# Expert weights of a PEER layer: half of the one-hot's product with the gate given to GpSimd

## The chip, the cores and the metric

The kernel runs on one core of one Trainium2 chip. The metric is the device time of one execution in microseconds (us); the time of a kernel is the median of its runs. The engines of the core are named as in the profile: PE (matrix products, with its weight loads as PEld), DVE (the vector engine), ACT (the scalar engine), POOL (GpSimd) and SP (which issues most of the DMAs). Each runs its own queue of instructions in order, and semaphores make one wait for another.

## The reference

One transformer block over 2048 tokens of width 448: layer norm, attention with 16 heads, a residual, then a second layer norm and a PEER layer (a mixture with one expert per row of `u` and `v`, 64 x 64 = 4096 experts). What matters here is the PEER layer:

```python
s1 = einsum("nhd,ed->nhe", q1, k1); s2 = einsum("nhd,ed->nhe", q2, k2)
i1 = argsort(-s1)[..., :8];  i2 = argsort(-s2)[..., :8]
cand = t1[..., :, None] + t2[..., None, :]          # 64 pairs per head
top_s, top_e = best 8 of cand, expert = i1 * 64 + i2
g = softmax(top_s)
act = gelu(einsum("nd,nhkd->nhk", xf, u[top_e]))
out = einsum("nhk,nhk,nhkd->nd", g, act, v[top_e])
```

So each token has 16 heads x 8 = 128 chosen experts, each with a gate.

## The kernel before

The kernel doesn't gather rows of `u` and `v`. It computes all 4096 expert activations of a token as dense products and multiplies them by a dense table of gates, `G`, that is zero where an expert wasn't chosen. The tokens go through the PEER layer in four batches of 512 (`b` = 0 to 3). For each batch:

- `up` (L1208 for its load, L100 for its 11 matmuls, L1221 for the GELU) computes the activations of 128 experts, `f` = 0 to 31.
- `weights` (L1019 to L1086) builds `G` for the batch.
- `weigh` (L1261, with L1267 to L1270) multiplies the activations by `G` and the scale and splits the product in two f16 parts; `experts` (L1273, matmuls on L1295) multiplies these by `v` into the four accumulators `acc`; `drain` (L1302, L1305) adds the residual and writes the batch out.

`weights` is the part around the change. The 128 chosen slots of a token lie on the partitions. A chosen expert has a number split in two: a row of 128 and a column of 32. The table of one token is then a product of two one-hot matrices over the slots: a 128-wide one, `p1`, and a 32-wide one, `f1`, whose ones are replaced by the gates. The gate is kept as a high f16 part (`k` = 0) and a low f16 part (`k` = 1), so there are two versions of the gated one, side by side in the tile `fg` with the shape [128, 16, 2, 32, 2]: pairs of tokens, part `k`, column, token of the pair.

The work goes in steps of 16 tokens (`TG`), and in groups of 32 (`TF`), two steps each. On DVE:

- `first(t)` (L1035) makes `f1` for a group by comparing the slots' columns with an iota; 1024 elements per partition. The tile has one buffer (tag `f1`).
- `factors(t, f1)` (L1041) multiplies `f1` by both parts of the gate, 2048 elements per partition, into `fg`, which has two buffers.
- `chosen(s)` (L1049) runs once a step. At the first step of a group it calls `factors`; at the second it calls `first` for the next group; in both it then makes `p1` for its step (L1056; 2048 elements, two buffers).

The loop of `weights` calls `chosen` one step ahead: at step `s` it first issues `chosen(s + 16)` and then the matmuls of step `s`. For batch 0 these are two matmuls of 32 columns per token (L1083), added up on PE, and ACT copies the result to `G` (L1085). For the batches 1 to 3 it is one matmul of 64 columns per token (L1073), and the two parts are added by ACT and DVE: ACT copies the high part from PSUM to `G` (L1076), and DVE adds the low part, read from PSUM, to it (L1077), twice a step.

The order around the change: batch 0 is woven with other work by hand (`weave` inside a `manual_schedule` block, L1228 on): the projection of batch 3, `kept_scores` (matmuls on L100 into the tile `M`, copies by ACT) and the first `up`s. For the later batches the program weaves `weights(b + 1)` in two parts. The first `2 + EARLY` pieces (`EARLY` is 11, 11 and 13 of the 32 steps) run beside the end of `experts(b)`; the rest runs beside 19 `up`s of the next batch and the `drain` of the last (L1322). There a planner orders the instructions of each engine, with some orders pinned (`issue_after`). `G` of a batch must be complete before its first `weigh` past the ones in flight, because each expert's slice takes all 512 tokens.

Of the kernel before, what the change touches and what calls it, by code (L numbers as in the profile page):

```python
# [12 lines left out]
F16 = mybir.dt.float16  # L13
# [3 lines left out]
OP = mybir.AluOpType  # L17
# [47 lines left out]
def block(ctx: ExitStack, tc: tile.TileContext, x, wqk, wv, wo, wq, k12, uT, v, cst, out):  # L65
    nc = tc.nc
# [931 lines left out]
    TG = 16  # L998
    TF = 32
# [16 lines left out]
    def of_tokens(b, c):  # L1016
        return G[:, :, TG * c:TG * c + TG] if b % 2 == 0 else G[:, c].rearrange("p (f t) -> p f t", t=TG)

    def weights(b, summed=(), name=lambda: "A"):  # L1019


        st = bg.tile([128, 2, 1024], F16, name="st", bufs=2)
        nc.sync.dma_start(st, s_d[b])
        slots, gslots = st[:, 0].rearrange("p (k n) -> p k n", k=2), st[:, 1].rearrange("p (t k u) -> p t k u", k=2, u=2)

        def pairs(k, t, m, n):
            return (slots[:, k, t:t + m].rearrange("p (t u) -> p t u", u=2).unsqueeze(2)
                    .to_broadcast([128, m // 2, n, 2]))

        def ids(m, n):  # L1030
            return iota2[:, :n].unsqueeze(1).to_broadcast([128, m // 2, n, 2])

        def first(t):
            f1 = bk.tile([128, TF // 2, 32, 2], F16, name="f1", tag="f1")
            nc.vector.tensor_tensor(f1, pairs(1, t, TF, 32), ids(TF, 32), op=OP.is_equal)  # L1035
            return f1

        def factors(t, f1):
            fg = gp.tile([128, TF // 2, 2, 32, 2], F16, name="fg", bufs=2)
            g = gslots[:, t // 2:t // 2 + TF // 2].rearrange("p t k u -> p (t k) u")  # L1040
            nc.vector.tensor_tensor(  # L1041
                fg.rearrange("p t k f u -> p t k (f u)"),
                f1.rearrange("p t f u -> p t (f u)").unsqueeze(2).to_broadcast([128, TF // 2, 2, 64]),
                g.unsqueeze(2).to_broadcast([128, TF, 32, 2]), op=OP.mult)
            return fg

        f1 = fg = None

        def chosen(s):  # L1049
            nonlocal f1, fg  # L1050
            if s % TF == 0:
                fg = factors(s, f1)
            elif s + TG < 512:
                f1 = first(s + TG)
            p1 = bk.tile([128, TG // 2, 128, 2], F16, name="p1", tag="p1", bufs=2)
            newest[0] = nc.vector.tensor_tensor(p1, pairs(0, s, TG, 128), ids(TG, 128), op=OP.is_equal).ins  # L1056
            return p1, fg

        yield
        f1 = first(0)  # L1060
        ahead = chosen(0)
        yield
        for s in range(0, 512, TG):
            p1, f = ahead
            if s + TG < 512:
                ahead = chosen(s + TG)
            dst = of_tokens(b, s // TG)
            if s // TG in summed:
                for h in range(0, TG, TG // 2):
                    ps = P[0].tile([128, TG // 2, 2, 32], F32, name=name())  # L1070
                    for t in range(TG // 2):
                        a, u = divmod(h + t, 2)
                        nc.tensor.matmul(ps[:, t], p1[:, a, :, u], f[:, s % TF // 2 + a, :, :, u], start=True, stop=True)  # L1073
                    hi, lo = (ps[:, :, k].rearrange("p t f -> p f t") for k in range(2))
                    d = dst[:, :, h:h + TG // 2]
                    nc.scalar.activation(d, hi, AF.Copy)  # L1076
                    nc.vector.tensor_tensor(d, lo, d, op=OP.add)  # L1077
            else:
                ps = P[0].tile([128, TG, 32], F32, name=name())
                for t in range(TG):  # L1080
                    a, u = divmod(t, 2)
                    for k in range(2):
                        nc.tensor.matmul(ps[:, t], p1[:, a, :, u], f[:, s % TF // 2 + a, k, :, u],  # L1083
                                         start=k == 0, stop=k == 1)
                nc.scalar.activation(dst, ps.rearrange("p t f -> p f t"), AF.Copy)  # L1085
            yield  # L1086
# [53 lines left out]
    with tc.manual_schedule(engines={ET.PE, ET.DVE, ET.Activation, ET.Pool, ET.SP}):  # L1140
# [31 lines left out]
        for b in range(3):  # L1172
            t = begin[b] - FOLDED
# [8 lines left out]
            else:  # L1182
                work += [(pipeline([pairs_of(j, nc.gpsimd) for j in (0, 1)], 6), 6 + PAIRS_POOL, t + 20, 257 - FOLDED)]
        w0 = weights(0)

        def first_tokens():
# [9 lines left out]
    gp = ctx.enter_context(tc.tile_pool(name="gp", bufs=1, side="right", reuse_waits="tile"))  # L1196
# [121 lines left out]
    for b in range(NB):  # L1318
        n = AHEAD if b else UP0
        if b:  # L1320
            tag[0] = "A"
            weave((ws, 32 - EARLY[b], 0, 1), (dr, 4, 0, 0.7), (ups(b, n), n, 0, 1))  # L1322
        acc = [pa.tile([128, 512], F32, name=f"acc{j}") for j in range(4)]
        work = [(experts(b, n, acc), 32, 0, 1)]
        if b == 0:
            tag[0] = "M"
            ws = weights(1, SUMMED[1], lambda: tag[0])
            work += [(islice(later, n), n, lo, hi) for n, lo, hi in ((2 * PAIRS, 0, 0.13), (32, 0.13, 0.6), (PLACES, 0.6, 0.72))]
            work += [(islice(ws, 2 + EARLY[1]), 2 + EARLY[1], 0.7, 1)]
        elif b < 3:  # L1330
            tag[0] = "M"
            ws = weights(b + 1, SUMMED[b + 1], lambda: tag[0])
            work += [(islice(later, LATER[b]), LATER[b], 0, SPLIT[b]), (islice(ws, 2 + EARLY[b + 1]), 2 + EARLY[b + 1], SPLIT[b] + 0.02, 1)]
        weave(*work)
        dr = drain(b, acc)
# [51 lines left out]
```

## Time and profile before

| | us |
|---|---|
| runs of the kernel before (three) | 1582.46, 1582.63, 1585.69 |
| median | 1582.63 |
| the profiled execution's own time | 1589.57 |
| its span in the profile | 1587.8 |

The profiled execution is 6.94 us above the median of the runs. All times within the trace are counted from the start of the span. By the trace, `weights` works on the four batches at these times, taken from the first and the last instruction on L1041: batch 0 from 829.5 to 914.6, batch 1 from 1036.9 to 1132.2, batch 2 from 1188.1 to 1296.1, batch 3 from 1350.9 to 1467.6. GpSimd's last instruction starts at 860.18 us; it does nothing in the rest of the kernel.

How to read it: the busy time of an engine says nothing by itself; what matters is which engine another one waits for in the stretch in question. The views of windows and of the chain of waits are therefore given stretch by stretch. A duration of an instruction is longer than the distance from its start to that of the next one on the same engine, since the end of one overlaps the start of the next; where DVE works without a pause, the distance between starts is what an instruction costs.

### The profile page before, as it was taken

To read this page: it belongs to the slowest core of one execution; us is meant where nothing else is said; L and a number is where in the kernel's file an instruction comes from. 1 tells how busy PE (TensorE), PEld (TensorE's weight loads), DVE (VectorE), ACT (ScalarE), POOL (GpSimd) and SP (SyncE) were. 2 spreads that over 40 slices of the span, in tenths; PEclk is the share of its full clock that TensorE was granted. 3 is DMA by queue.
4 is the path that set the end of the run, shared out by engine and by line. 5 is a ranking of instruction groups with operands and counts; after the bars stand their busy time and mean duration, and the time that the engine had idled before them with its cause. 6 is when DMAs were issued, how large, how long until landed. Compare 5 with 4: busy or idle time off the path is not lost.

```text
span 1587.8 us, 33145 instructions
## 1 busy us (share of the span) xinstructions
PE 1528.4 (96%) x12441; PEld 647.1 (41%) x12441; DVE 1168.6 (74%) x3944; ACT 907.6 (57%) x1220; POOL 360.4 (23%) x484
## 2 busy tenths in 40 slices
PE   5999999999999999999998999999999999999998
PEld 3444222222332233222335644455445554555444
DVE  7763355565667767666698999799998998889623
ACT  3544888898888888987863422334323343333321
POOL 1242000524245753796570000000000000000000
PEclk9999999999999999999999999999999999999999
DMA  8424688669965757678642244454344434443454
GB/s 277 141 98 127 220 270 262 203 196 296 298 214 160 202 180 226 197 199 270 222 139 89 72 145 129 130 179 117 107 136 137 150 98 148 130 136 113 121 144 134
DMA packets 176474, 270.36 MB, mean 170 GB/s; under 512 B 29948, under 2 KB 106492, under 8 KB 176312
## 3 DMA queue, kind: packets, MB, share of 16 engines
q1 hardware_dynamic: 172088, 266.14, 55.0%
q10 hardware_dynamic: 4224, 2.10, 0.5%
q8 instruction: 97, 1.59, 0.4%
q14 instruction: 65, 0.53, 0.1%
HBM read 215.91 MB, written 49.50 MB: 167 GB/s over the span
## 4 chain that ended last, share of the span: by engine, by line
PE 70%; DVE 22%; DMA 3%; POOL 2%; issue 2%; ACT 1%; SPq 0%; DVEq 0%; POOLq 0%; ACTq 0%
PE acc L1295 13%; PE A L652 13%; PE M L100 12%; PE S L574 11%; PE A L100 9%; PE pq L100 6%; DVE p L1056 4%; DVE G L1077 2%; DVE fg L1041 2%; PE M L280 2%; DVE ring L1267 1%; DVE pos L880 1%; DVE w L1270 1%; DVE f L1035 1%; PE A L1083 1%
## 5 line engine op out<-in xcount | busy, mean ns | idle before, releaser
L578 ACT ACTIVATE P<-S,escale 128x1024 f32<-128x1024 f32 x512 | 533.0, 1123 | 72.0 <-PE S L574 65.9
L1295 PE MATMUL acc<-v,w 128*128 128x448 f16 x1536 | 308.3, 354 | 1.3 <-DVE w L1270 1.0
L652 PE MATMUL A<-P,V 128*32 128x512 f32 x2048 | 258.4, 603 | 0.0
L574 PE MATMUL S<-qS,kS 32*128 32x512 f16 x3072 | 238.1, 381 | 2.7 <-ACT P L578 2.0
L1295 PEld LDWEIGHTS <-w 128*128 128x128 f16 x1536 | 148.4, 98 | 143.1 <-DVE w L1270 4.0
L100 PEld LDWEIGHTS <-u 128*128 128x128 f16 x1386 | 131.1, 98 | 146.4 <-issue 6.8
L100 PE MATMUL A<-Xb,u 128*128 128x512 f16 x759 | 178.6, 384 | 2.5 <-DVE G L1077 2.5
L100 PE MATMUL M<-w,Xb 128*128 128x512 f16 x704 | 166.2, 383 | 8.7 <-DVE Xb L144 4.8
L1221 ACT ACTIVATE ring<-A,ugelu 128x512 f32<-128x512 f32 x71 | 48.6, 686 | 219.4 <-PE A L100 219.4
L1056 DVE TENSOR_TENSOR p<-st,iota 128x2048 f16<-128x2048 f16 x128 | 157.5, 1231 | 15.0 <-PE M L1073 8.1
L574 PEld LDWEIGHTS <-kS 32*128 32x128 f16 x3072 | 65.7, 92 | 214.9 <-issue 177.7
L1267 DVE SCALAR_TENSOR_TENSOR ring<-ring,wscale,G 128x512 f32<-128x512 f32 x128 | 93.9, 766 | 77.2 <-ACT ring L1221 77.1
L100 PE MATMUL M<-Xb,u 128*128 128x512 f16 x627 | 146.3, 379 | 0.0
L100 PEld LDWEIGHTS <-Xb 128*128 128x128 f16 x704 | 64.0, 98 | 99.8 <-issue 26.5
L878 DVE MAX8 ti<-fresh 128x8 f32<-128x64 f32 x384 | 57.4, 215 | 58.9 <-ACT fresh L859 58.7
L1269 ACT ACTIVATE w<-ring 128x512 f16<-128x512 f32 x128 | 75.9, 622 | 40.8 <-DVE ring L1267 28.6
L652 PEld LDWEIGHTS A<-P,V 128*32 128x32 f32 x2048 | 48.1, 109 | 122.5 <-issue 114.8
L1270 DVE SCALAR_TENSOR_TENSOR w<-w,ring 128x512 f16<-128x512 f16 x128 | 86.5, 698 | 7.2 <-ACT w L1269 6.9
L1113 POOL TENSOR_SCALAR raw<-raw,scale 128x512 f32<-128x512 f32 (+1 forms) x64 | 44.9, 702 | 200.9 <-DMA raw<-in_uT_dram 199.9
L1221 ACT ACTIVATE ring<-M,ugelu 128x512 f32<-128x512 f32 x57 | 39.2, 687 | 88.2 <-PE M L100 86.5
L1041 DVE TENSOR_TENSOR fg<-f,st 128x2048 f16<-128x2048 f16 x64 | 78.5, 1227 | 0.1
L880 DVE FIND_INDEX8 ti<-ti,fresh 128x8 uint32<-128x64 f32 x384 | 77.5, 226 | 0.0
(209 smaller groups left out, 1904.3 us busy)
## 6 DMA issues: line engine op xcount, KB each, us to landing
v<-vs SPq DMA_DIRECT2D x128, 336.0 KB
u<-us SPq DMA_DIRECT2D x126, 256.0 KB
w<-wp SPq DMA_DIRECT2D x56, 512.0 KB
kS<-ks SPq DMA_DIRECT2D x64, 256.0 KB
V<-vd SPq DMA_DIRECT2D x64, 256.0 KB
wr<-in_wq_dram SPq DMA_DIRECT2D x32, 448.0 KB
vs<-hl SPq DMA_DIRECT2D x32, 336.0 KB
seen<-in_uT_dram SPq DMA_DIRECT2D x32, 256.0 KB
```

The source lines that it names most:

```text
L100: nc.tensor.matmul(ps, l, r, start=i == 0, stop=i == len(pairs) - 1)
L574: nc.tensor.matmul(S[j // 2][:, j % 2], kS[r, a, 128 * (k % 4):128 * (k % 4) + 128], qS[r, c], start=m == 0, stop=m == 2)
L578: nc.scalar.activation(Pt[:, 2 * i:2 * i + 2], S[i], AF.Exp, scale=escale[:, n % 4:n % 4 + 1])
L652: nc.tensor.matmul(O[n][32 * j:32 * j + 32], V[:, k % 4, j], Pt[:, j], start=k == 0, stop=k == NT - 1)
L880: nc.vector.max_index(i, t, src)
L1041: nc.vector.tensor_tensor(fg.rearrange("p t k f u -> p t k (f u)"), f1.rearrange("p t f u -> p t (f u)").unsqueeze(2).to_broadcast([128, T ...
L1056: newest[0] = nc.vector.tensor_tensor(p1, pairs(0, s, TG, 128), ids(TG, 128), op=OP.is_equal).ins
L1221: gelu[0] = nc.scalar.activation(act, p, AF.Gelu_apprx_tanh, scale=ugelu).ins
L1267: nc.vector.scalar_tensor_tensor(av, av, wscale, of_expert(b, f), op0=OP.mult, op1=OP.mult)
L1269: nc.scalar.activation(w[:, 0], a, AF.Copy, scale=1.0 / LS)
L1270: newest[0] = nc.vector.scalar_tensor_tensor(w[:, 1], w[:, 0], -LS, a, op0=OP.mult, op1=OP.add).ins
L1295: nc.tensor.matmul(acc[j][:, :D], l, r, start=f == 0 and k == 0, stop=f == 31 and k == 2)
```

## The change

From some group on, `fg` of a group is made in two halves by two engines. At the first step of a group, `chosen` no longer calls `factors` for it, if the half of GpSimd is already under way: DVE then multiplies `f1` by the high part alone (1024 elements), and at once makes `f1` of the next group (which was done at the second step), allocates the next `fg` tile, and GpSimd is given the product of this `f1` with the low part of the gate. So GpSimd has a whole group, 32 tokens, before the next half of DVE comes. For batch 0 this begins with the group at token 160, for the others with the group at token 32: 11 + 3 x 15 = 56 of the 64 groups. `f1` still has one buffer, `fg` two.

```diff
+        def half(fg, t, f1, k, eng):
+            g = gslots[:, t // 2:t // 2 + TF // 2, k]
+            eng.tensor_tensor(fg[:, :, k], f1, g.unsqueeze(2).to_broadcast([128, TF // 2, 32, 2]), op=OP.mult)
+
         f1 = fg = None
+        shared = {}
 
         def chosen(s):
             nonlocal f1, fg
             if s % TF == 0:
-                fg = factors(s, f1)
-            elif s + TG < 512:
+                if s in shared:
+                    fg = shared.pop(s)
+                    half(fg, s, f1, 0, nc.vector)
+                else:
+                    fg = factors(s, f1)
+                n = s + TF
+                if n < 512 and (b or n >= 160):
+                    f1 = first(n)
+                    shared[n] = gp.tile([128, TF // 2, 2, 32, 2], F16, name="fg", bufs=2)
+                    half(shared[n], n, f1, 1, nc.gpsimd)
+            elif s + TG < 512 and s + TG not in shared:
                 f1 = first(s + TG)
```

## The prediction

> **What bounds the kernel now.** The page's busy row first, then the windows in which the trace has `weights` at work, then for each of them the chain of waits that ended last.
>
> ```profile
> PE 1528.4 (96%) x12441; PEld 647.1 (41%) x12441; DVE 1168.6 (74%) x3944; ACT 907.6 (57%) x1220; POOL 360.4 (23%) x484
> ```
> ```profile
> 866.00:918.00 52.00, 50.15 (x912) 33.25 (x912) 47.97 (x48) 22.69 (x36) 0.00 (x0) 1.00 0.37 123
> 1036.00:1075.00 39.00, 36.31 (x344) 20.56 (x342) 38.38 (x57) 14.25 (x36) 0.00 (x0) 1.00 0.53 167
> 1075.00:1131.00 56.00, 55.59 (x519) 29.89 (x515) 56.00 (x85) 25.23 (x58) 0.00 (x0) 1.00 0.41 118
> 1220.00:1265.00 45.00, 44.21 (x408) 24.84 (x407) 41.63 (x64) 17.16 (x41) 0.00 (x0) 1.00 0.50 152
> 1265.00:1302.00 37.00, 35.55 (x339) 19.24 (x336) 35.20 (x54) 15.22 (x38) 0.00 (x0) 1.00 0.40 111
> 1370.00:1418.00 48.00, 48.00 (x380) 26.28 (x377) 37.38 (x57) 16.86 (x38) 0.00 (x0) 1.00 0.46 129
> 1418.00:1445.00 27.00, 23.75 (x222) 13.00 (x220) 23.70 (x37) 9.57 (x23) 0.00 (x0) 1.00 0.49 146
> 1445.00:1480.00 35.00, 35.00 (x327) 19.09 (x327) 29.63 (x47) 14.67 (x36) 0.00 (x0) 1.00 0.33 91
> ```
>
> The columns of a window are its length and the busy time of PE, PEld, DVE, ACT and POOL, then PE's granted clock and the DMA. The page's 96% of PE isn't the answer: in the windows of `weights` DVE is as full as PE, and POOL does nothing. Who is waited for is said by the chains, here for 866 to 918 (batch 0), 1075 to 1131 (batch 1 beside the `up`s), 1265 to 1302 (batch 2) and 1420 to 1480 (batch 3):
>
> ```profile
> by line: PE M L100 49.5%; PE A L1083 27.9%; DVE p L1056 15.7%; DVE fg L1041 4.4%; DVE f L1035 2.3%; DVE Xb L144 0.6%; issue 0.2%
> ```
> ```profile
> by line: DVE p L1056 36.8%; DVE G L1077 24.2%; DVE fg L1041 20.1%; DVE f L1035 9.6%; DVE ht L1305 4.2%; issue 3.5%; DVE cand L904 2.0%
> ```
> ```profile
> by line: DVE p L1056 27.6%; DVE G L1077 15.6%; PE M L100 12.8%; DVE fg L1041 12.3%; DMA out_dram<-ht 10.0%; DMA ht<-h 7.0%; DVE f L1035 6.5%; DVE ht L1305 3.8%; PE A L1073 3.7%; issue 1.0%
> ```
> ```profile
> by line: PE M L100 43.5%; DMA ht<-h 12.0%; DMA out_dram<-ht 11.0%; PE A L1073 9.4%; DVE p L1056 5.7%; DVE G L1077 5.3%; DVE ht L1305 4.4%; DVE ring L1267 3.5%; issue 2.7%; DVE fg L1041 1.9%; ACT ring L1221 1.1%; DVE f L1035 1.0%; ACT G L107
> ```
>
> Batches 1 and 2 are bound by DVE, batch 0 by PE with DVE only 4.0 us short of full (52.00 - 47.97), batch 3 mostly by PE. PE is nearly full everywhere, so DVE time taken away is worth little: PE's idle time is 1.85 us in batch 0, 2.69 + 0.41 in batch 1 and 0.79 + 1.45 in batch 2, some 7 us in all. DVE time added is worth nearly all of itself in batches 1 and 2.
>
> **What the change takes from DVE.** The DVE timeline of one group of batch 1:
>
> ```profile
> 1097.51 1.25 DVE L1041 TENSOR_TENSOR fg<-f,st 128x2048 f16<-128x2048 f16 x1
> 1098.64 1.25 DVE L1056 TENSOR_TENSOR p<-st,iota 128x2048 f16<-128x2048 f16 x1
> 1099.78 0.78 DVE L1077 TENSOR_TENSOR G<-A,G 128x256 f32<-128x256 f32 x2
> 1100.44 0.71 DVE L1305 SCALAR_TENSOR_TENSOR ht<-acc,oscale,ht 128x448 f32<-128x448 f32 x1
> 1101.03 0.71 DVE L1035 TENSOR_TENSOR f<-st,iota 128x1024 f16<-128x1024 f16 x1
> 1101.63 1.25 DVE L1056 TENSOR_TENSOR p<-st,iota 128x2048 f16<-128x2048 f16 x1
> 1102.77 0.78 DVE L1077 TENSOR_TENSOR G<-A,G 128x256 f32<-128x256 f32 x2
> 1103.43 1.25 DVE L1041 TENSOR_TENSOR fg<-f,st 128x2048 f16<-128x2048 f16 x1
> ```
>
> From start to start `fg` costs 1.13 us, `p` 1.14, a pair of `G` adds 0.66 and `f`, of 1024 elements, 0.60. DVE's half has 1024 elements of the same type, so I take 0.60 for it: 0.53 saved per group, in 56 groups 30 us of DVE time. `first` only moves from the second step to the first. No DMA moves, and POOL has nothing else to do by then.
>
> **What it adds on POOL.** Its half is a two-input product of 1024 f16 elements. The nearest rows of POOL, one operation of the same size and two smaller ones, the last with a broadcast operand as here:
>
> ```profile
> L939 POOL TENSOR_TENSOR sel<-sel 128x1024 f16<-128x1024 f16 x10 | 21.3, 2132 | 0.7
> L939 POOL TENSOR_TENSOR sel<-sel 128x512 f16<-128x512 f16 x10 | 12.5, 1253 | 0.7
> L935 POOL TENSOR_TENSOR sel<-sel,iv 128x256 f16<-128x256 f16 x80 | 53.5, 696 | 75.9 <-DVE sel L931 75.9
> ```
>
> I take 2.13 us, the same size. Bounds: 1.76 from the slope between the first two (0.879 us for 512 elements), 2.8 from the last (four times 0.696). A group lasts 4.0 us on DVE in batch 0 (2 x 1.14 + 1.13 + 0.60) and 5.3 in the others (two pairs of adds more), so POOL is in time by itself.
>
> **What POOL's work costs DVE** decides the sign. The trace has both engines at work together before 835 us; the POOL rows start with a 1024-element product (2.13 of the 4.42 and of the 4.49):
>
> ```profile
> 546.56 4.42 POOL L939 TENSOR_TENSOR sel<-sel 128x1024 f16<-128x1024 f16 x3
> 546.62 2.12 DVE L135 CAST hl<-xn 128x64 f16<-128x64 f32 x1
> L135 DVE CAST hl<-xn x12: 181/538/2121, 345.3 to 719.8; 128x64 f16<-128x64 f32 x12
> 824.45 4.49 POOL L939 TENSOR_TENSOR sel<-sel 128x1024 f16<-128x1024 f16 x3
> 825.92 0.75 DVE L644 SCALAR_TENSOR_TENSOR on<-M,onscale,on 128x512 f32<-128x512 f32 x1 [1.27 <-PE M L643]
> 828.34 1.15 DVE L1035 TENSOR_TENSOR f<-st,iota 128x1024 f16<-128x1024 f16 x1
> ```
>
> A cast of 64 elements, 0.18 us at its fastest, began 0.06 us behind POOL's product and ended with it: it stood still for the whole 2.1 us. `f` itself took 1.15 where its neighbours take 0.7. But L644, which reads one operand from PSUM (`M`), ran its 0.75 us unslowed, all but the last 0.1 of it under the other product (824.45 to 826.58). So I take it that a POOL product holds up the DVE instructions that read all from SBUF (`p`, `f`, both halves), for all of its time, and not the `G` adds, which read the low part from PSUM.
>
> The Trainium skill ("SBUF — State Buffer", Who interferes with whom) states this as an exclusive lock on a shared pair of ports, held for the full instruction, which a `tensor_tensor` with both inputs in SBUF contends for with GpSimd's reads. By it the sum is the one below; the cast's row agrees with it.
>
> Now where POOL starts. Its half waits for `f` of its group and for PE to have read the buffer of two groups before; DVE in turn gets one wait, that of the next `f` for POOL's half, since `f` has one buffer. In the order of the new code DVE issues half, `f`, `p`, two adds, `p`, two adds. `p` follows `f` at once, while POOL must first be told that `f` is done: `p` goes first, POOL starts at its end, the two adds (0.66) run beside it, and the next `p` stands 2.13 - 0.66 = 1.47 us. In batch 0 there are no adds on DVE, and a full 2.13 stands. Per group: +1.47 - 0.53 = **+0.94 us** in batches 1 to 3, +2.13 - 0.53 = **+1.60 us** in batch 0. Behind a standing `p` wait the rest of DVE's queue, PE's matmuls of that step and ACT's copies.
>
> The slack that takes some of it, DVE's idle time:
>
> ```profile
> L1056 DVE TENSOR_TENSOR p<-st,iota 128x2048 f16<-128x2048 f16 x24 | 29.2, 1221 | 4.0 <-PE A L1083 4.0
> 1429.56 0.68 DVE L1305 SCALAR_TENSOR_TENSOR ht<-acc,oscale,ht 128x448 f32<-128x448 f32 x1 [2.06 <-DMA ht<-h]
> 1454.36 1.22 DVE L1056 TENSOR_TENSOR p<-st,iota 128x2048 f16<-128x2048 f16 x1 [0.27 <-PE A L1073]
> ```
>
> - Batch 0: 11 x 1.60 = 17.6, less the 4.0 that DVE waits for PE in that window: **+13.5**.
> - Batch 1: 15 x 0.94 = 14.1; DVE has 0.6 us idle, and four `ht` instructions (0.59 each, reading `acc` from PSUM) can lie beside POOL: **+13**.
> - Batch 2: the first 4 or 5 groups, before 1245, have 3.4 us idle in the first window (45.00 - 41.63), which takes theirs; the other 10 give 10 x 0.94 = 9.4: **+10** with a little for the rest.
> - Batch 3: to 1418 the idle time of DVE (10.6 of 48) takes all. Behind that 8 groups give 7.5, against 3.3 + 5.4 us idle by the windows, of which some stand at the end, where no group is: **+3**.
>
> Sum +39.5 us. The profiled execution, 1589.6 us with 1587.8 of span, would be 1629; it lay 6.9 above the median of the runs, and I put the same sum on the median: 1582.6 + 39.5 = **1622 us**.
>
> **The ends.** With 1.76 instead of 2.13, the 44 or so groups that count (11 + 15 + 10 + 8) cost 0.37 less each: -16, 1606. With 2.8: +0.67 each, +30, 1652.
>
> **Rivals.**
>
> - *POOL works beside DVE for nothing* (faster). For it: L644 above wasn't slowed. Against: the cast was. Then 0.53 us a group goes from DVE, PE becomes the bound in batches 1 and 2, and its 7 us of idle time is all there is to gain: 1576. It decides where POOL's hold per group falls below 0.53 + 0.66, 1.2 us. The Trainium skill ("Perfetto Trace Analysis", Optimizing Scalar/DVE Operations) speaks for this one, that offloading some work to Scalar or even GPSIMD may make sense if DVE is saturated, and warns in the same place that the two share a read port.
> - *The hold finds cover*: the planner orders the later batches anew, so that POOL's product lies under both pairs of adds (1.33) or under DVE's waits for PE and `ht`. Then a group costs 2.13 - 1.33 - 0.53 = +0.27, 25 to 30 groups some 7 us, and batch 0, ordered by hand, between 0 and 8: 1583 to 1597.
> - *POOL is slower than 2.13*, because of its pattern (pairs of gates repeated 32 times) or because `p`s keep it waiting, so that DVE also waits for it at the next `f`, whose one buffer it still reads: 1652 by the bound above, to 1680.
>
> **Chances.** Forecast (1600 to 1640) 0.60; slower POOL (1640 to 1680) 0.15; cover (1583 to 1597) 0.12, half of it within 0.2%; for nothing (1572 to 1579) 0.13. About 0.2%, 3 us, is what a measurement of this kernel can tell from no change. So faster 0.13, same 0.06, slower 0.81. The range from 1583 to 1655 leaves out the faster case and the far end of the slower POOL.
>
> **What would show it.** Right: `p`, `f` and the halves on DVE with durations up to 2 us longer in one of every two steps, none for the adds; POOL with 56 products of about 2.13 us from start to end, more where it was kept waiting; DVE full in 866 to 918, and the batch 0 window longer by 13 us. Wrong: these DVE lines at 1.22 and 0.69 beside a busy POOL (the first rival); POOL's products under the adds alone (the second); DVE waiting for POOL by semaphore at L1035 (the third).

## The result and the profile after

The changed kernel takes 1626.46 us (median of 5 runs, 1624.84 to 1628.55) against 1584.86 us (median of 5, 1582.46 to 1588.88): 1.0267 times as long, with a 95% interval of 1.0253 to 1.0281, or +41.6 us. The forecast was 1622 in a range of 1583 to 1655.

The lines have moved: `p` is now on L1070 (it was L1056), the `G` adds on L1091 (L1077), the matmuls into `G` on L1087 and L1097 (L1073 and L1083), both halves of `fg` on L1049. The page's busy row of the changed kernel, whose profiled execution took 1625.46 us, and two of its groups:

```profile
PE 1531.3 (94%) x12441; PEld 647.4 (40%) x12441; DVE 1212.6 (75%) x3944; ACT 909.3 (56%) x1220; POOL 507.8 (31%) x540
...
L1049 POOL TENSOR_TENSOR fg<-f,st 128x1024 f16<-128x1024 f16 x56 | 146.8, 2621 | 503.7 <-DVE f L1035 244.7
...
L1070 DVE TENSOR_TENSOR p<-st,iota 128x2048 f16<-128x2048 f16 x128 | 189.3, 1486 | 15.4 <-PE A L1087 6.9
```

DVE was to be relieved of 30 us and is busy for 44 us more (1212.6 against 1168.6), with the same number of instructions. `p`, which the change doesn't touch, went from 1231 ns to 1486.

Where the time came from, in windows cut at the same events of both kernels: from the last undivided `fg` of batch 0 to the first matmul into `acc`, from the first `fg` of batch 1 to the first `acc` of batch 1, then on to the first `acc` of the batches 2 and 3. Before, then after (length, then busy time of PE, PEld, DVE, ACT, POOL):

```profile
866.20:923.50 57.30, 55.48 (x958) 35.77 (x959) 52.58 (x64) 24.76 (x40) 0.00 (x0) 0.97 0.36 122
1036.90:1137.85 100.95, 95.86 (x879) 52.15 (x878) 100.29 (x152) 41.68 (x96) 0.00 (x0) 0.98 0.44 132
1137.85:1308.10 170.25, 166.24 (x1250) 87.54 (x1248) 159.72 (x399) 58.06 (x128) 0.00 (x0) 1.00 0.46 131
1308.10:1480.90 172.80, 167.33 (x1260) 88.81 (x1260) 145.38 (x277) 64.41 (x140) 0.00 (x0) 0.99 0.44 128
```
```profile
859.70:928.50 68.80, 58.97 (x958) 36.88 (x959) 66.21 (x64) 24.75 (x40) 29.52 (x11) 0.93 0.30 101
1041.90:1157.65 115.75, 97.90 (x879) 52.01 (x877) 111.25 (x152) 41.06 (x96) 38.60 (x16) 0.99 0.37 115
1157.65:1338.80 181.15, 168.20 (x1249) 87.73 (x1249) 170.12 (x399) 59.84 (x129) 37.27 (x14) 1.00 0.41 123
1338.80:1516.85 178.05, 169.02 (x1260) 88.79 (x1260) 155.11 (x277) 65.35 (x140) 41.38 (x15) 0.99 0.41 124
```

| batch | longer | DVE busy more | DVE idle more | forecast |
|---|---|---|---|---|
| 0 | 11.5 | 13.6 | -2.1 | 13.5 |
| 1 | 14.8 | 11.0 | +3.8 | 13 |
| 2 | 10.9 | 10.4 | +0.5 | 10 |
| 3 | 5.3 | 9.7 | -4.5 | 3 |
| sum | 42.5 | 44.7 | -2.3 | 39.5 |

(Idle time is the length less the busy time. One product of batch 2 lies in batch 1's window, which is why POOL has 16 there and 14 in the next.) The two spans differ by 35.9 us only (1623.7 less 1587.8). The other 6.5 lie ahead of the first window, where the kernels do the same: that window begins 6.5 us earlier in the changed kernel's trace.

What became of PE: in batch 0 the chain that ended last had 49.5% PE M L100 and 15.7% `p`. In the changed kernel, for 868 to 923 and, below it, for 1080 to 1148 (batch 1):

```profile
by line: DVE p L1070 52.2%; PE M L100 18.6%; DVE fg L1049 10.1%; PE A L1097 8.0%; DVE f L1035 7.5%; issue 7.0%; DVEq L1035 0.2%
```
```profile
by line: DVE p L1070 35.6%; DVE G L1091 17.2%; DVE fg L1049 12.6%; issue 12.4%; DVE f L1035 9.8%; PE M L100 7.2%; PE A L1087 4.1%; DVE ht L1319 1.8%; DVEq L1035 0.1%; DVEq L1319 0.0%
```

DVE is now the bound in batch 0 too. The granted clock in that window was 0.93 against 0.97, and the same matmuls kept PE busy for 3.5 us more; how much of the 11.5 us comes from that wasn't separated. One group there, DVE and then POOL:

```profile
892.45 0.68 DVE L1049 TENSOR_TENSOR fg<-f,st 128x1024 f16<-128x1024 f16 x1
893.23 0.69 DVE L1035 TENSOR_TENSOR f<-st,iota 128x1024 f16<-128x1024 f16 x1
893.84 4.07 DVE L1070 TENSOR_TENSOR p<-st,iota 128x2048 f16<-128x2048 f16 x2
897.83 0.68 DVE L1049 TENSOR_TENSOR fg<-f,st 128x1024 f16<-128x1024 f16 x1
```
```profile
894.06 2.76 POOL L1049 TENSOR_TENSOR fg<-f,st 128x1024 f16<-128x1024 f16 x1 [2.62 <-DVE f L1035]
```

Two `p` take 2.35 us elsewhere; here 4.07. The first goes through, since it began before POOL was told of `f`; POOL's record begins at 894.06 and is 2.76 long, because it has to wait for that `p` (to about 894.9) and then works for 1.9; the second `p` stands until POOL is done. A group takes 5.38 us from half to half, where it took 4.0 when DVE didn't wait.

A group of batch 1, and one of batch 3, with the POOL product of each:

```profile
1097.90 0.67 DVE L1049 TENSOR_TENSOR fg<-f,st 128x1024 f16<-128x1024 f16 x1
1098.50 1.21 DVE L1070 TENSOR_TENSOR p<-st,iota 128x2048 f16<-128x2048 f16 x1
1099.63 0.68 DVE L1035 TENSOR_TENSOR f<-st,iota 128x1024 f16<-128x1024 f16 x1
1100.23 0.74 DVE L1091 TENSOR_TENSOR G<-A,G 128x256 f32<-128x256 f32 x2
1100.90 2.55 DVE L1070 TENSOR_TENSOR p<-st,iota 128x2048 f16<-128x2048 f16 x1
```
```profile
1100.45 1.91 POOL L1049 TENSOR_TENSOR fg<-f,st 128x1024 f16<-128x1024 f16 x1 [4.22 <-DVE f L1035]
```
```profile
1495.02 1.23 DVE L1070 TENSOR_TENSOR p<-st,iota 128x2048 f16<-128x2048 f16 x1 [0.49 <-PE A L1087]
1496.16 0.75 DVE L1091 TENSOR_TENSOR G<-A,G 128x256 f32<-128x256 f32 x2
1496.83 1.74 DVE L1049 TENSOR_TENSOR fg<-f,st 128x1024 f16<-128x1024 f16 x1
```
```profile
1495.07 2.95 POOL L1049 TENSOR_TENSOR fg<-f,st 128x1024 f16<-128x1024 f16 x1 [3.68 <-PE A L1087]
```

In batch 1 the planner has put `p` ahead of `f`, so that POOL starts beside the adds. These read the low part from PSUM and keep their 0.74 us (for the two); the next `p` takes 2.55 instead of 1.21: it stands until POOL's product ends, at 1102.36, and ends 1.09 us behind that. In batch 3 POOL and `p` begin at the same release from PE, `p` wins, POOL's record is 2.95 long (1.04 of waiting and 1.91 of work), the adds run free, and DVE's own half stands: 1.74 instead of 0.68.

### The profile page after: what moved, and what is told of

Its sections match the earlier page's. It is cut to its first block, busy times and chain, and to the rows that moved or that the text cites. A ratio compares the mean times of both kernels' runs of the same rounds, so it can differ in the third digit from the quotient of the medians.

```text
span 1623.7 us, 33323 instructions
## 1 busy us (share of the span) xinstructions
PE 1531.3 (94%) x12441; PEld 647.4 (40%) x12441; DVE 1212.6 (75%) x3944; ACT 909.3 (56%) x1220; POOL 507.8 (31%) x540
## 3 DMA queue, kind: packets, MB, share of 16 engines
q1 hardware_dynamic: 172088, 266.14, 53.4%
## 4 chain that ended last, share of the span: by engine, by line
PE 61%; DVE 27%; DMA 4%; POOL 3%; issue 3%; ACT 1%; SPq 0%; DVEq 0%; POOLq 0%; ACTq 0%
PE acc L1309 12%; PE A L652 11%; PE M L100 10%; PE S L574 10%; PE A L100 7%; DVE p L1070 7%; PE pq L100 5%; DVE fg L1049 3%; DVE G L1091 2%; DVE ring L1281 2%; DVE f L1035 2%; DVE w L1284 2%; PE M L280 2%; DVE pos L880 1%; PE A L1087 1%
## 5 line engine op out<-in xcount | busy, mean ns | idle before, releaser
L1049 POOL TENSOR_TENSOR fg<-f,st 128x1024 f16<-128x1024 f16 x56 | 146.8, 2621 | 503.7 <-DVE f L1035 244.7
L1070 DVE TENSOR_TENSOR p<-st,iota 128x2048 f16<-128x2048 f16 x128 | 189.3, 1486 | 15.4 <-PE A L1087 6.9
L100 PEld LDWEIGHTS <-u 128*128 128x128 f16 x1386 | 131.1, 98 | 146.1 <-issue 5.1
L100 PE MATMUL A<-Xb,u 128*128 128x512 f16 x759 | 176.0, 380 | 1.6 <-DVE G L1091 1.6
L100 PE MATMUL M<-w,Xb 128*128 128x512 f16 x704 | 166.9, 385 | 8.8 <-DVE Xb L144 4.8
L1281 DVE SCALAR_TENSOR_TENSOR ring<-ring,wscale,G 128x512 f32<-128x512 f32 x128 | 95.1, 769 | 75.1 <-ACT ring L1235 75.1
L100 PE MATMUL M<-Xb,u 128*128 128x512 f16 x627 | 146.9, 382 | 0.0
L100 PEld LDWEIGHTS <-Xb 128*128 128x128 f16 x704 | 64.4, 99 | 100.9 <-issue 28.3
L878 DVE MAX8 ti<-fresh 128x8 f32<-128x64 f32 x384 | 56.9, 209 | 56.2 <-ACT fresh L859 55.9
L1284 DVE SCALAR_TENSOR_TENSOR w<-w,ring 128x512 f16<-128x512 f16 x128 | 91.7, 737 | 5.6 <-ACT w L1283 5.3
L1087 PEld LDWEIGHTS <-p 128*128 128x128 f16 x1536 | 61.1, 97 | 63.8 <-issue 27.2
```

Source lines behind the costliest of these rows:

```text
L100: nc.tensor.matmul(ps, l, r, start=i == 0, stop=i == len(pairs) - 1)
L1049: eng.tensor_tensor(fg[:, :, k], f1, g.unsqueeze(2).to_broadcast([128, TF // 2, 32, 2]), op=OP.mult)
L1281: nc.vector.scalar_tensor_tensor(av, av, wscale, of_expert(b, f), op0=OP.mult, op1=OP.mult)
L1284: newest[0] = nc.vector.scalar_tensor_tensor(w[:, 1], w[:, 0], -LS, a, op0=OP.mult, op1=OP.add).ins
```

## The experiments

The theory: POOL's product holds up every DVE instruction that reads all its operands from SBUF, for as long as POOL works. The rivals: (A) the new order on DVE, with `f` at the first step and `fg` in two pieces, costs the time; (B) PE or DVE waits by semaphore for POOL's half. The diffs are against the changed kernel.

**e1: the same split, no POOL.**

```diff
-                    half(shared[n], n, f1, 1, nc.gpsimd)
+                    half(shared[n], n, f1, 1, nc.vector)
```

> The structure of the change stays (f of the next group made at the first step, fg in two halves), but DVE makes both halves, 0.60 us each; POOL gets nothing. Theory (POOL's product holds the DVE instructions that read all from SBUF): the hold is gone, DVE works 2 x 0.60 - 1.13 = 0.07 us more per group than before, 1585 to 1590 us. Rival A (the new order of f and p on DVE, and the low part of fg coming in a separate instruction, cost the time): it stays, 1615 to 1630. Rival B (PE or DVE waits for POOL's half by semaphore): 1585 to 1590 too, so this run does not tell B from the theory.

Measured: 1598.79 us, 1.009 of the time before (1.0061 to 1.012): less than rival A's, but some 9 us above the theory's. The expectation missed a wait. In its trace, for 862 to 934 (batch 0):

```profile
L1070 DVE TENSOR_TENSOR p<-st,iota 128x2048 f16<-128x2048 f16 x24 | 28.2, 1217 | 0.0
L1049 DVE TENSOR_TENSOR fg<-f,st 128x1024 f16<-128x1024 f16 x22 | 15.1, 687 | 16.6 <-PE A L1097 16.1
```

`p` is free (1217 ns), but DVE stands 16.6 us in front of `fg`: the half of the group ahead needs a buffer that PE still reads, and when DVE makes that half itself, DVE has to wait for it. In the change POOL does that waiting. This left open whether the order adds anything, for which e5 was made.

**e2: POOL writes, but reads nothing.** POOL sets the low half to zero, so the gates' low part is left out.

```diff
-                    half(shared[n], n, f1, 1, nc.gpsimd)
+                    nc.gpsimd.memset(shared[n][:, :, 1], 0.0)
```

> POOL writes zeros into the low half of fg instead of the product, so the low part of the gates is left out; the order on PE, DVE, ACT and SP is that of the changed kernel. POOL's instruction then writes the same 1024 elements but reads nothing, and no longer waits for f. Theory, with the hold coming from POOL's reads of SBUF: p, f and the half on DVE at their free durations (1.22, 0.69, 0.69), the 0.53 us per group saved is left and PE becomes the bound: 1575 to 1582 us, which is also the most that the change could give with a free POOL. If a POOL write holds DVE as well: about 1 us per group held, less 0.66 under the adds, 1583 to 1592. Rival A (order): 1615 to 1630, since the order is the same.

Measured: 1575.63 us, 0.9946 (0.993 to 0.9963), with the order of all the other engines that of the changed kernel. Groups by form from 820 us on, of the changed kernel and of e2:

```profile
L1070 DVE TENSOR_TENSOR p<-st,iota 128x2048 f16<-128x2048 f16 x128 | 189.3, 1486 | 15.4 <-PE A L1087 6.9 <-PE M L1087 6.7 <-PE A L1097 1.5
L1281 DVE SCALAR_TENSOR_TENSOR ring<-ring,wscale,G 128x512 f32<-128x512 f32 x128 | 95.1, 769 | 75.1 <-ACT ring L1235 75.1
L1284 DVE SCALAR_TENSOR_TENSOR w<-w,ring 128x512 f16<-128x512 f16 x128 | 91.7, 737 | 5.6 <-ACT w L1283 5.3
L1049 DVE TENSOR_TENSOR fg<-f,st 128x1024 f16<-128x1024 f16 x56 | 65.7, 1173 | 0.1
L1091 DVE TENSOR_TENSOR G<-A,G 128x256 f32<-128x256 f32 x122 | 45.5, 413 | 5.1 <-ACT G L1090 5.1
```
```profile
L1070 DVE TENSOR_TENSOR p<-st,iota 128x2048 f16<-128x2048 f16 x128 | 155.6, 1221 | 27.1 <-PE M L1087 11.1 <-PE A L1087 8.3 <-PE A L1097 7.2
L1281 DVE SCALAR_TENSOR_TENSOR ring<-ring,wscale,G 128x512 f32<-128x512 f32 x128 | 91.8, 742 | 79.5 <-ACT ring L1235 79.4
L1284 DVE SCALAR_TENSOR_TENSOR w<-w,ring 128x512 f16<-128x512 f16 x128 | 84.8, 683 | 5.8 <-ACT w L1283 5.5
L1091 DVE TENSOR_TENSOR G<-A,G 128x256 f32<-128x256 f32 x122 | 45.5, 414 | 5.0 <-ACT G L1090 5.0
...
L1049 DVE TENSOR_TENSOR fg<-f,st 128x1024 f16<-128x1024 f16 x56 | 38.1, 681 | 0.1
...
L1066 POOL MEMSET fg<- 128x1024 f16 x56 | 53.4, 954 | 543.3 <-PE M L1087 320.8 <-PE A L1087 144.6 <-PE A L1097 42.0
```

The same instructions in the same order are free beside 56 POOL instructions of 0.95 us that don't read. These do lie beside `p`: 41.8 of their 53.4 us overlap with a `p`. One such pair, POOL and DVE:

```profile
1089.49 0.95 POOL L1066 MEMSET fg<- 128x1024 f16 x1 [4.76 <-PE A L1087]
```
```profile
1089.55 1.22 DVE L1070 TENSOR_TENSOR p<-st,iota 128x2048 f16<-128x2048 f16 x1
```

The differences in the mean durations add up to the hold: 128 x 0.265 for `p`, 56 x 0.492 for the half, 128 x 0.027 and 128 x 0.054 for L1281 and L1284 give 33.9 + 27.6 + 3.5 + 6.9 = 71.9 us, 1.28 per product. The adds, with 413 against 414, have none of it. Rival A falls, since the order is here and the time isn't. And 1575.6 is what the whole idea could be worth, 7.9 us, if POOL's work were free: behind that PE is the bound (busy for 165.9 of the 169.5 us of batch 2 in e2, DVE for 153.6).

**e3: POOL's product beside, for nobody.** DVE makes both halves when the group is used; POOL makes the product into a tile that isn't read.

```diff
-                    half(fg, s, f1, 0, nc.vector)
+                    for k in range(2):
+                        half(fg, s, f1, k, nc.vector)
...
-                    half(shared[n], n, f1, 1, nc.gpsimd)
+                    half(gp.tile([128, TF // 2, 2, 32, 2], F16, name="again", bufs=1), n, f1, 1, nc.gpsimd)
```

> DVE makes both halves of fg (0.60 each), and POOL makes the same product as in the change, into a tile of its own that nothing reads. Nobody needs POOL's result; only the next f must wait until POOL has read the last one. Theory: the hold is all there and nothing is saved, so the changed kernel's time plus 0.60 us for each of the 45 or so groups that count: 1645 to 1660 us. Rival B (waits for POOL's half): 1585 to 1595, since nobody waits for it. Rival A (order): 1615 to 1630.

Measured: 1649.79 us, 1.041 (1.0379 to 1.0441). The time is there although neither PE nor the halves depend on POOL, so rival B falls. From 820 us on the waits of DVE for POOL by semaphore are 1.0 us:

```profile
L1035 DVE TENSOR_TENSOR f<-st,iota 128x1024 f16<-128x1024 f16 x64 | 44.1, 689 | 5.3 <-DMA st<-sd 2.7 <-POOL again L1049 1.0 <-DVE fg L1049 0.5
```

Not all of the extra time is the products', though. Between 800 and 850 us, ahead of the first of them, PE stands for a load that it doesn't wait for in the changed kernel:

```profile
PEld L100 <- DMA ring<-us: 10.1, 1, 10.1
```

Only the two runs with the extra tile `again` have this wait (9.9 us in e4). The tile comes from the same pool as `ring`; that it moves `ring` to memory which comes free later is likely, but no run shows it.

**e4: POOL's product twice.**

```diff
                     half(shared[n], n, f1, 1, nc.gpsimd)
+                    half(gp.tile([128, TF // 2, 2, 32, 2], F16, name="again", bufs=1), n, f1, 1, nc.gpsimd)
```

> The changed kernel, with POOL's product made twice per group, the second time into a tile that nothing reads. Theory: a second hold of 1.9 us per group; the first lies 0.66 us under adds as before, the second finds the other pair of adds at best (0.66) and stands 1.25 to 1.9 otherwise: with 45 to 56 groups +55 to +105, 1680 to 1730 us. Rival A (order): 1620 to 1635. Rival B (POOL late): two products are 3.8 us of a group of 6.1, still in time, 1626 to 1640.

Measured: 1699.83 us, 1.0722 (1.0689 to 1.0754). That is 73.4 us more than the changed kernel. Of the 77.3 us between the two profiled spans, 15.0 lie ahead of the last undivided `fg` of batch 0, where the load is waited for as in e3; in the four windows the second product costs 62.3 us, 1.11 each, against the 1.28 of hold that the first has. Some of it is a new wait: `f` now stands 9.4 us for POOL in all (6.6 and 2.8 by its two products).

**e5: e3 without POOL.**

```diff
-                    half(fg, s, f1, 0, nc.vector)
+                    for k in range(2):
+                        half(fg, s, f1, k, nc.vector)
...
-                    half(shared[n], n, f1, 1, nc.gpsimd)
```

> As e3, without POOL's product: DVE makes both halves of fg at the first step of their group (not a group ahead, as in e1), and f of the next group right behind them. Nothing is on POOL and no half is made before PE has let go of its buffer. Theory: 2 x 0.60 - 1.13 = 0.07 us per group, 1585 to 1590 us, so e3's extra time over this is POOL's hold alone, 60 us. Rival A (the new order of f and p costs something by itself): 1598 or more, like e1. What e1 had over the forecast would then be the order; if this one is at 1585 to 1590, it was DVE's wait for PE's buffer (21.7 us idle in front of fg in e1's trace).

Measured: 1581.1 us, 0.999 (0.9976 to 1.0003): no difference from the kernel before, some 4 us under the expectation. The order of `f` and the cut of `fg` in two cost nothing, and what e1 had on top was its wait for PE's buffer. Against this control e3 is 68.7 us longer. By the two traces, with 70.4 us between the spans, 13.5 lie ahead of the first window and 56.9 in the four windows: 1.02 for each of the 56 products.

**e6: POOL reads one operand.** It copies `f` into the low half, so the one-hot stands where the gate's low part should.

```diff
-                    half(shared[n], n, f1, 1, nc.gpsimd)
+                    nc.gpsimd.tensor_copy(shared[n][:, :, 1], f1)
```

> POOL copies f into the low half of fg instead of multiplying, so the gate's low part is replaced by the one-hot; the order on PE, DVE, ACT and SP is that of the changed kernel. POOL reads one operand of 1024 elements instead of two; from its cast of 512 (0.61 us) about 1.1 us. Theory: the hold is as long as POOL's instruction: 1.1 - 0.66 - 0.53 = about -0.1 us per group in batches 1 to 3, 1.1 - 0.53 = +0.57 in batch 0 less 4 us of idle time, 1580 to 1590 us. If a POOL instruction with one input doesn't hold DVE: 1574 to 1578, as e2.

Measured: 1588.73 us, 1.0041 (1.0027 to 1.0056). POOL's fastest copy took 1.04 us, hardly longer than e2's memset (0.95; the copies' median is 1.90, since a record holds the wait for a `p`), and the order on the other engines is the same, yet it costs 13.1 us more: `p` is at 1346 ns instead of 1221, the half at 769 instead of 681:

```profile
L1070 DVE TENSOR_TENSOR p<-st,iota 128x2048 f16<-128x2048 f16 x128 | 171.2, 1346 | 17.5 <-PE M L1087 8.8 <-PE A L1087 6.7 <-PE A L1097 1.7
L1049 DVE TENSOR_TENSOR fg<-f,st 128x1024 f16<-128x1024 f16 x56 | 43.1, 769 | 0.1
```

In all DVE is busy for 23.2 us more than in e2 (1167.1 against 1143.9), 0.41 per copy.

**e7: half the size.** POOL makes the low part of 16 tokens of the group, DVE that of the other 16.

```diff
+                    half(fg, s, f1, 1, nc.vector, slice(TF // 4, TF // 2))
...
-                    half(shared[n], n, f1, 1, nc.gpsimd)
+                    half(shared[n], n, f1, 1, nc.gpsimd, slice(0, TF // 4))
```

> POOL makes the low part for 16 of the group's 32 tokens (512 elements) and DVE, in an instruction of its own (0.33 us), for the other 16. Theory: POOL's product is about 1.0 us, of which 0.66 lies under the adds; DVE saves 1.13 - 0.60 - 0.33 = 0.2: +0.14 us per group in batches 1 to 3, +0.8 in batch 0 less 4 us: 1588 to 1602 us. Rival (a fixed cost per POOL instruction, as that of the hand-over, whatever its length): the hold stays and the saving is smaller, 1635 to 1645.

Measured: 1595.35 us, 1.0081 (1.0061 to 1.01), inside the theory's range. POOL's fastest product of 512 elements took 1.05 us. The cost goes with the length of POOL's instruction beyond what the adds cover, not with the number of its instructions.

**e8: batch 0 alone.**

```diff
-                if n < 512 and (b or n >= 160):
+                if n < 512 and not b and n >= 160:
```

> Only the 11 groups of batch 0 from token 160 on are shared; the batches 1 to 3 are as before. Theory: batch 0 gives its part of the whole and no more: between its 8.8 us in the changed kernel's trace and the 13.5 of the prediction, 1592 to 1597 us. If what happens in batch 0 is made up later, 1584; if the batches 1 to 3 cost nothing by themselves, 1626.

Measured: 1594.18 us, 1.0083 (1.006 to 1.0106), +10.8 us, where the windows above give batch 0 11.5. Batch 0's loss is still there at the end; nothing of it is made up later.

No version with POOL's product beat the kernel before, and e5 only equals it. e2 shows how little there is to find: 7.9 us is all there is to gain, and 1.28 us of hold stand against 0.53 saved per group.

## Why the prediction was right

- **Who bounds** was read rightly: freeing DVE in the same order (e2) gave 7.9 us, forecast 7, and PE took over; in batch 1 the two are then about equally full (93.1 and 92.4 of 95.9 us).
- **The saving**, 0.53 us a group: DVE's half costs 0.60 from start to start (1097.90 to 1098.50), as taken from `f`.
- **POOL's product**: taken as 2.13 from the row of the same size, it was 1.91 at its fastest; its mean of 2.62 holds the wait for a `p`. The lower bound, 1.76, was nearer than the upper, 2.8: with the repeated gates it took no longer than the plain product of that size. Fastest, median and slowest of the changed kernel:

```profile
L1049 POOL TENSOR_TENSOR fg<-f,st x56: 1909/2764/2958, 862.5 to 1501.7; 128x1024 f16<-128x1024 f16 x56
```

- **The hold**: whole, as the cast's row had shown, and none for the adds. Per product it was forecast at 2.13 in batch 0 and 1.47 elsewhere, 11 x 2.13 + 45 x 1.47 = 89.6 us in all; it was 71.9. The size of POOL's product explains most of it: with 1.91 in batch 0 and 1.91 - 0.66 = 1.25 in the others it would be 77.3.
- **Where POOL starts**: as forecast in batch 0 (behind a `p`). In batch 1 the planner turned `p` and `f` round, so that POOL starts beside the adds; their 0.66 cover is the same either way.
- **The slack** is the term that was wrong. The forecast let DVE's idle time, and the `ht` instructions, take 59.9 - 39.5 = 20.4 us of the gross loss (59.9, the 89.6 of hold less 29.7 of saving). In the windows DVE's idle time shrank by 2.3 us: by 2.1 and 4.5 in batches 0 and 3 as against 4.0 and 11 in the forecast, while batch 1 got 3.8 us of new idle time, mostly for PE. DVE's waits in its window, before and then after:

```profile
DVE p L1056 <- PE M L1073: 0.5, 1, 0.5
```
```profile
DVE p L1070 <- PE A L1087: 2.4, 3, 1.4
DVE f L1035 <- POOL fg L1049: 1.1, 1, 1.1
DVE p L1070 <- PE M L1087: 0.5, 1, 0.5
```

  A `p` that stands makes PE late, and DVE waits for PE at a later `p`, whose buffer PE still reads. That idle time between two engines which wait for each other comes back in this way, and so isn't free for a third one's hold, is my reading; no run separates it.
- So the sum, 39.5 against 41.6 measured, came out closer than its terms: the hold was some 18 us too large, the slack some 18 us too large as well, and the two cancelled. The direction and the mechanism were foreseen; that the time was met within 2 us is luck.
- The rival *POOL works beside DVE for nothing* is what e2 shows for a POOL that doesn't read, at the time given for it (1576 against 1575.6). The rival *the hold finds cover* didn't come; its near relative is e7, where a shorter product lies largely beside the adds. The rival of a POOL so slow that DVE waits for it by semaphore shows once in batch 1 (1.1 us) and began in earnest only in e4.

## What to carry to other kernels

Before work is moved from DVE to POOL, look at what DVE runs beside it: while POOL reads, DVE instructions that read both operands from SBUF stand (`p`, both halves, L1281 and L1284 here), and those that read one from PSUM pass. The price per moved piece is POOL's duration less the PSUM-reading DVE work that lies directly beside it, and this has to be below what DVE saves; here 1.28 against 0.53. On the mean that isn't enough: e6's copies cost DVE 0.41 each, less than 0.53, and the kernel was still 5.4 us slower than before. In batch 0 no adds cover the copy, so that 1.04 stands against 0.53 there, and the window of batch 0 was 3.0 us longer; that of batch 2 was 2.2 us longer too, which this doesn't explain. So the price is to be taken stage by stage. And a full engine isn't yet worth relieving: the next bound, PE, was 8 us away, whatever POOL had cost.

## What the runs showed of the hardware

- A POOL memset of 0.95 us doesn't hold DVE at all, a POOL copy of 1.04 us does (e2 and e6, same order of all else). The Trainium skill ("SBUF — State Buffer", Who interferes with whom) has this: a DVE instruction with two SBUF inputs contends with a GpSimd instruction that reads SBUF, not with one that only writes it. The traces agree, 1221 ns for `p` in e2 against 1346 in e6.
- POOL's record begins before its work does: 2.95 us for a product of 1.91 that first stood behind a `p` (batch 3 above). Its mean duration of 2.62 us would overstate the hold.
- The stretch ahead of the change, the same in both kernels, differed by 6.5 us between the two profiled executions. For 815 to 866 us the granted clock was 0.90 before and 0.97 after, but e5, with 0.90 there as well, has its last undivided `fg` of batch 0 at 859.8, as early as the changed kernel (859.7). So the clock of that stretch doesn't explain it, and the cause stays open.
